# Logs of the gates split into three bfloat16 numbers by GpSimd, their running sums in bfloat16 passes, and the gates' steps moved ahead of the masks

## The chip, the core and the metric

The kernel runs on one core of one Trainium2 chip. The metric is the time of one execution in microseconds on the device, the median of three runs. Everything is computed on one TensorE (matmuls and transposes), one VectorE, one ScalarE and one GpSimd, each with an instruction stream of its own that is worked off in order; the SP queue issues most of the transfers.

## The reference

The first half is a gated linear recurrence with 4 batches, 8 heads, 768 steps and heads of 48:

```python
f = 1.0 / (1.0 + np.exp(-f_logit))
for t in range(S):
    state = f[:, :, t, :, None] * state + np.einsum('bhd,bhe->bhde', k[:, :, t], v[:, :, t])
    y[:, :, t] = np.einsum('bhd,bhde->bhe', q[:, :, t], state)
```

The second half takes y as 3072 rows of 384 and routes each row through two levels of gates (4 groups of 4 experts, both by argmax) to one of 16 experts, relu(x @ w1) @ w2 with a hidden width of 1024, scaled by the product of the two softmax weights:

```python
g_idx = np.argmax(x @ w_group, axis=1)
e_idx = np.argmax(xg @ w_expert[g], axis=1)          # rows xg of group g
out[tok_idx] = combined[:, None] * (np.maximum(xg[mask_e] @ w1[g, e], 0.0) @ w2[g, e])
```

## The kernel before

**The scan.** The 768 steps are cut into 6 chunks of 128, and the 4 batches into 2 pairs. A chunk of one pair of batches is a *unit*; there are 12 of them, numbered 0 to 11, `units[i] = (c, s)`. Each unit goes through stages, each a generator whose `yield`s cut it into steps: `bounded` (c) bounds the gate logits on VectorE; `gated` (g) turns them into logs on ScalarE (an exponential and a log of 128x768, in place, tile ld_f) and then, in two batches (b = 0, 1), forms the running sum of the logs within the chunk on TensorE, a matmul of 128x384 with the triangle of ones `tri` as the stationary operand (tile cs, line 600), and from it two exponentials on ScalarE, eq and kh (lines 601 and 602). The last row of eq is sent by GpSimd's queue to the small tile ends (line 607). `multiplied` (m) multiplies q by eq and k by kh on VectorE (lines 620 and 623); `turned` (t) transposes both on TensorE; `scored` (s) makes the scores ap and masks them on VectorE with `tri` (line 663, four instructions of 128x512, "the masks"); `stated` (n) updates the state (ds, sp, st); `weighed` (w) makes the output y from the state and the masked scores; `done` (d) takes the router's logits lT and lg from it; `listed` (x) transposes the output back to rows; `decayed` (b) turns ends into the decays of a chunk (gt). `routed` (r) ranks the rows of a finished chunk: small VectorE instructions, the matmuls rk and tb, and a transfer (meta, line 246) by GpSimd's queue.

**The order.** TensorE, VectorE, ScalarE and SP run in exactly the order in which the program issues their instructions (`manual_schedule`); only GpSimd's instructions are ordered by the framework. The order is written out as words: `c+2` means the next step of stage c of unit i+2. BEGIN is the order up to unit 2 and the first part of unit 4, and then each of i = 3 to 12 runs through EVEN or ODD, or through an order of its own in ORDERS (the last four). In EVEN and ODD the two sums of unit i+1 stand at `g+1 g+1`, the score steps of unit i at `s s s s`, and the bound, exponential and log of unit i+2 at `c+2`, `g+2` and `g+2`. An iteration of the steady part is about 10.5 to 11.3 us long in the profile.

**After the scan.** Two experts are worked on while the scan ends (`early`), and then the experts one after another: gathered rows, transposes, `up` (hp, line 439), `down` (yo, line 475) and scattered rows. The change does not touch this part.

Of the kernel before, what the change touches and what calls it, by code (L numbers as in the profile page):

```python
# [10 lines left out]
FP32 = mybir.dt.float32  # L11
I32 = mybir.dt.int32
U32 = mybir.dt.uint32
BF16 = mybir.dt.bfloat16
AF = mybir.ActivationFunctionType
OP = mybir.AluOpType
AX = mybir.AxisListType.X
ET = mybir.EngineType
P = 128
# [4 lines left out]
def kernel(  # L24
# [12 lines left out]
    nc = tc.nc  # L37
    B, H, S, D = q.shape
# [38 lines left out]
    def const(shape, dtype, name):  # L77
        return cp.tile(shape, dtype, tag=name, name=name)

    def bank(shape, name):  # L80
        return ps.tile(shape, FP32, tag="bank", name=name)
# [8 lines left out]
    tri = const([P, P], FP32, "tri")  # L90
    ident = const([P, P], FP32, "ident")
    strictb = const([P, P], BF16, "strictb")
    onesb = const([P, P], BF16, "onesb")
    halves = const([P, 2], FP32, "halves")
    make_upper_triangular(nc, tri, val=1.0, diag=True)
    make_identity(nc, ident)
    nc.vector.memset(onesb, 1.0)
    nc.vector.tensor_tensor(strictb, tri, ident, OP.subtract)

# [286 lines left out]
    def fetch(pool, rows, n, top=N, late=False):  # L388

        w = {"n": n, "pool": pool, "early": top < N, "late": late, "blocks": [(j, min(P, n - j * P)) for j in range((n + P - 1) // P)]}  # L390
        w["x"] = pool.tile([P, len(w["blocks"]), RW], FP32, tag="xg", bufs=2 if pool is ep else 6, name="xg")
        for j, m in w["blocks"]:
            nc.gpsimd.indirect_dma_start(out=w["x"][:, j, :], out_offset=None, in_=x_dram[0:1 + top, :], in_offset=bass.IndirectOffsetOnAxis(ap=rows[:, j:j + 1], axis=0))  # L393
        return w
# [124 lines left out]
    with ExitStack() as fast:  # L519
        sb = fast.enter_context(tc.tile_pool(name="sb", bufs=2))  # L520
# [26 lines left out]
        NU = len(units)  # L547
# [9 lines left out]
        def side(i):  # L557


            return nc.gpsimd if i < NU - 2 else nc.scalar  # L560
# [3 lines left out]
        def parts(i):  # L564

            return (slice(0, 1), slice(1, 2)) if i == 0 else (slice(0, 2),)
# [10 lines left out]
        def bounded(i):  # L577
# [3 lines left out]
                nc.vector.tensor_scalar(f, f, -44.0, None, OP.max)  # L581
            yield

        def gated(i):

            c, s = units[i]
            w = live[i]

            nl = w["f"].rearrange("p b h d -> p b (h d)")
            for b in parts(i):  # L590
                nc.scalar.activation(nl[:, b], nl[:, b], AF.Exp, bias=0.0, scale=-1.0)
                if i:
                    yield
                nc.scalar.activation(nl[:, b], nl[:, b], AF.Ln, bias=1.0, scale=1.0)  # L594
            eq, qh, kh = pads["eq"][i % 2], w["qh"], pads["kh"][i % 3]
            w.update(eq=eq, kh=kh)
            yield
            for b in range(2):
                cs = bank([P, H, D], "cs")
                nc.tensor.matmul(cs.rearrange("t h d -> t (h d)"), lhsT=tri, rhs=nl[:, b], start=True, stop=True)  # L600
                nc.scalar.activation(eq[:, b, :, 0:D], cs, AF.Exp, bias=0.0, scale=-1.0)  # L601
                nc.scalar.activation(kh[:, b, :, 0:D], cs, AF.Exp, bias=0.0, scale=1.0)
                if b:

                    if s == 0:
                        ends[c] = sb.tile([B, H * DP], FP32, tag="ends", bufs=1, name="ends")
                    side(i).dma_start(out=ends[c][2 * s:2 * s + 2, :], in_=eq[P - 1:P].rearrange("o b h d -> o b (h d)"))  # L607
                yield
# [171 lines left out]
        def advance(gens):  # L780
# [6 lines left out]


        STAGES = {"c": bounded, "g": gated, "m": multiplied, "t": turned, "s": scored, "n": stated, "w": weighed, "d": done, "x": listed, "b": decayed}
        BEGIN = """c0 h g0 p g0 g0 m0 m0 m0 m0 l2 t0 t0 t0 t0 c1 g1 g1 s0 s0 s0 s0 g1 g1 p w0 w0 n0 m1 m1 m1 m1 l3 h x0 x0 x0  # L790
            t1 t1 t1 t1 b1 c2 g2 g2 s1 s1 s1 s1 p d0 g2 g2 n0 n1 w1 w1 m2 m2 l4 n1
            d0 x1 x1 t2 t2 t2 t2 c3 g3 g3 x1 s2 s2 s2 s2 w2 g3 g3 d1 w2 n2 m3 m3 c4 g4 g4""".split()
        BEGUN = 3
        EVEN = "l+2 d-2 n-1 r r r x-1 x-1 t t t t g+1 g+1 x-1 r s s s s c+2 w d-1 g+2 w g+2 n m+1 m+1".split()
        ODD = "l+2 d-2 r r x-1 x-1 t t t t b n-1 g+1 g+1 x-1 r s s s s c+2 w d-1 g+2 w g+2 n m+1 m+1 r n".split()
        ORDERS = {
            NU - 3: "l+2 o d-2 r r x-1 x-1 t t t t b n-1 r g+1 g+1 x-1 r s s s s c+2 w d-1 g+2 w g+2 n m+1 m+1 r n".split(),
            NU - 2: "d-2 r x-1 x-1 r t t t t r g+1 g+1 x-1 s s s s w d-1 w n m+1 m+1".split(),
            NU - 1: "d-2 r r n-1 x-1 x-1 t t t t r x-1 r s s s s w b d-1 w r r".split(),
            NU: "d-2 r e d-1 x-1 x-1 d-1 x-1 r r r e e r e r r e r r e r e r r e e e e e".split(),  # L800
# [3 lines left out]
        def step(nm, i):  # L804
            if nm == "r":
                advance(routes)
            elif nm == "e":
                next(first[0], None)
            elif nm == "p":
                next(pad)  # L810
            elif nm == "o":
                send_kept()
            elif nm == "h":
                next(turning)
            elif 0 <= i < NU:
                if nm == "l":

                    load(i, ("k", "qh"))
                    if i + 1 < NU:
                        load(i + 1, ("f",))  # L820
                    load(i, ("v",))
                    return
                if (nm, i) not in steps_of:
                    steps_of[nm, i] = STAGES[nm](i)
                next(steps_of[nm, i], None)
# [11 lines left out]
        for i in range(BEGUN, NU + 1):  # L837
            if i == BEGUN:
                nc.sync.dma_start(out=x_dram[0:1, 0:DM].rearrange("o (h d) -> o h d", d=D), in_=blank[:, 0:D].unsqueeze(1).broadcast_to((1, H, D)))
                nc.sync.dma_start(out=x_dram[0:1, DM:RW], in_=blank[:, D:D + 2])  # L840
            for tok in ORDERS.get(i, ODD if i % 2 else EVEN):
                step(tok[0], i + int(tok[1:] or 0))
# [62 lines left out]
    for n in range(GE - 1):  # L905
        w = ws[n]
# [105 lines left out]
    with tc.If(more > 0), ExitStack() as late:  # L1012
# [5 lines left out]
        with tc.For_i(0, last, 1) as i:  # L1018
# [14 lines left out]
            w = fetch(ep, row, P, late=True)  # L1033
# [32 lines left out]
```

## Time and profile before

| | us |
|---|---|
| median of 3 runs | 418.97 (418.01 to 419.13) |
| the profiled execution | 418.8 |
| span of the profile | 416.9 |
| TensorE busy | 404.8 (97%) |
| VectorE busy | 266.9 (64%) |
| ScalarE busy | 157.0 (38%) |
| GpSimd busy | 83.3 (20%) |
| matmuls of the running sums (line 600) | 48 passes, 19.7 |

How to read it: PE is TensorE's matmuls, PEld its loads of the stationary operand, DVE VectorE, ACT ScalarE, POOL GpSimd. A float32 matmul shows as two passes, so the 24 sums are 48 rows. The busy slices cut the span into 40 equal parts of 10.4 us; a digit is the busy share in tenths. In the timeline a row is a start in us, a length in us, the engine, the line, the operation, the output and inputs by their names, and in brackets how long the engine had been idle and on whom it waited. The chain of waits follows the end of the program back from what released it to what released that.

### The profile page before, as it was taken

Reading aid. Unit: us, or ns where it says so; the run is one execution under the profiler, and the core shown is the slowest. Engines: PE = TensorE matmul, PEld = TensorE weight load, DVE = VectorE, ACT = ScalarE, POOL = GpSimd, SP = SyncE. Lnnn points to the kernel's source line nnn. Section 1 sums busy time; section 2 is a strip of 40 time slices with the busy share of each in tenths; the row PEclk is TensorE's granted clock in tenths of the full one; section 3 lists DMA queues with packets and bytes.
Section 4 is the critical chain, followed back from the end, with each engine's and each line's share of the span. In section 5 each row is a group of like instructions: output and inputs, shape, how many; then the busy total and the mean of one; then the engine's idle time right before and its main releaser. Section 6 shows DMA issues by size and latency. Waiting matters only on the chain.

```text
span 416.9 us, 10083 instructions
## 1 busy us (share of the span) xinstructions
PE 404.8 (97%) x4055; PEld 376.0 (90%) x4055; DVE 266.9 (64%) x778; ACT 157.0 (38%) x353; POOL 83.3 (20%) x127
## 2 busy tenths in 40 slices
PE   5999999999999999999999999999999999999995
PEld 3888888888878878989999999999999999999992
DVE  5666787878898641550699777495595595594240
ACT  5777766666565412211122131231231231231220
POOL 4000010101012047101041321311322221120230
PEclk9999999999999999999999999999999999999998
DMA  9999997877999739976639476586595696585010
GB/s 166 203 204 203 184 175 140 154 148 156 257 321 382 260 112 360 381 276 232 227 119 326 118 277 232 178 326 181 199 340 138 261 316 194 210 321 161 28 47 25
DMA packets 132121, 88.98 MB, mean 213 GB/s; under 512 B 102630, under 2 KB 122700, under 8 KB 132066
## 3 DMA queue, kind: packets, MB, share of 16 engines
q1 hardware_dynamic: 125666, 75.50, 61.8%
q0 software_dynamic: 5792, 11.92, 9.7%
q10 hardware_dynamic: 608, 0.83, 0.6%
q8 instruction: 34, 0.56, 0.5%
q14 instruction: 21, 0.17, 0.1%
HBM read 78.71 MB, written 9.83 MB: 212 GB/s over the span
## 4 chain that ended last, share of the span: by engine, by line
PE 48%; issue 30%; DMA 9%; POOL 6%; DVE 3%; ACT 2%; POOLq 1%
PE hp L439 12%; PE yo L475 6%; DMA out_dram<-yt,xg 6%; PE y L702 5%; PE ap L660 4%; PE cs L600 4%; PE yo L460 4%; POOL out_dram L450 4%; PE x_ps L743 2%; POOL xg L393 2%; PE tr_q L634 2%; PE tr_k L634 2%; PE ds L677 2%; PE y L698 2%; DMA xg<-x_dram,rows_e 2%
## 5 line engine op out<-in xcount | busy, mean ns | idle before, releaser
L439 PE MATMUL hp<-xe,w 128*128 128x128 f32 (+14 forms) x864 | 138.6, 320 | 0.0
L439 PEld LDWEIGHTS hp<-xe,w 128*128 128x128 f32 x864 | 135.8, 190 | 0.8
L475 PE MATMUL yo<-h,w 128*128 128x230 f32 (+13 forms) x672 | 115.8, 333 | 0.0
L422 DVE STREAM_TRANSPOSE yr<-yT 32x192 f32<-32x192 f32 (+1 forms) x208 | 70.5, 339 | 70.4 <-ACT yT L476 67.8
L475 PEld LDWEIGHTS yo<-h,w 128*128 128x128 f32 x672 | 113.7, 190 | 0.2
L415 DVE STREAM_TRANSPOSE xe<-xg 32x192 f32<-32x192 f32 (+1 forms) x208 | 69.7, 335 | 8.6 <-PE hp L439 5.6
L440 ACT ACTIVATE h<-hp 128x256 f32<-128x256 f32 (+14 forms) x72 | 34.4, 478 | 103.6 <-PE hp L439 103.6
L450 POOL DMA_INDIRECT out_dram<-yt,xg x32 | 34.4, 1075 | 151.3 <-ACT yt L447 145.7
L476 ACT COPY yT<-yo 128x230 f32<-128x230 f32 (+13 forms) x42 | 13.4, 325 | 80.5 <-PE yo L475 80.5
L393 POOL DMA_INDIRECT xg<-x_dram,rows_p x30 | 29.7, 988 | 50.6 <-DMA out_dram<-yt,xg 27.6
L663 DVE TENSOR_TENSOR am<-ap,tri 128x512 f32<-128x512 f32 x48 | 29.8, 681 | 13.3 <-PE ap L660 13.3
L702 PE MATMUL y<-am,v 128*64 128x128 f32 x384 | 24.7, 277 | 0.7 <-issue 0.6
L702 PEld LDWEIGHTS y<-am,v 128*64 128x64 f32 x384 | 20.9, 137 | 4.1 <-issue 2.9
L660 PE MATMUL ap<-Tq,Tk 48*64 48x128 f32 x768 | 23.8, 272 | 0.2 <-ACT Tk L635 0.2
L660 PEld LDWEIGHTS ap<-Tq,Tk 48*64 48x64 f32 x768 | 20.8, 133 | 2.0 <-issue 1.1
L460 PE MATMUL yo<-w,h 128*128 128x384 f32 x64 | 21.3, 486 | 0.0
L600 PE MATMUL cs<-ld_f,tri 128*128 128x384 f32 x48 | 19.7, 536 | 0.4 <-ACT ld_f L594 0.2
L460 PEld LDWEIGHTS yo<-w,h 128*128 128x128 f32 x64 | 11.9, 190 | 7.4
L607 POOL DMA_DIRECT2D ends<-eq x10 | 5.4, 541 | 57.3 <-ACT eq L601 57.3
L447 ACT ACTIVATE yt<-yr,xg 128x384 f32<-128x384 f32 (+13 forms) x26 | 14.4, 604 | 5.4 <-DVE yr L422 5.4
L634 PE MATMUL tr_q<-ident,qh 128*128 128x128 f32 x96 | 15.4, 286 | 0.2 <-DVE qh L620 0.2
L705 ACT COPY xT<-y 128x512 f32<-128x512 f32 x24 | 13.5, 581 | 5.5 <-PE y L702 5.4
(171 smaller groups left out, 367.5 us busy)
## 6 DMA issues: line engine op xcount, KB each, us to landing
w<-in_moe_w_dram SPq DMA_DIRECT2D x34, 1536.0 KB, 10.6
qh<-in_q_dram SPq DMA_DIRECT2D x12, 384.0 KB, 5.0
ld_k<-in_k_dram SPq DMA_DIRECT2D x12, 384.0 KB, 5.9
v<-in_v_dram SPq DMA_DIRECT2D x12, 384.0 KB, 5.9
ld_f<-in_f_logit_dram SPq DMA_DIRECT2D x11, 384.0 KB, 5.7
x_dram<-x_kept SPq DMA_DIRECT2D x2, 1536.0 KB, 11.7
x_dram<-x POOLq DMA_DIRECT2D x2, 384.0 KB, 8.0
x_dram<-x ACTq DMA_DIRECT2D x2, 384.0 KB, 8.6
```

The costliest lines, as they stand in the source:

```text
L393: nc.gpsimd.indirect_dma_start(out=w["x"][:, j, :], out_offset=None, in_=x_dram[0:1 + top, :], in_offset=bass.IndirectOffsetOnAxis(ap=rows ...
L415: squares(w, lambda n, k_, rk, g, rg: nc.vector.transpose(out=xT[rg, 0:n, k_], in_=x[rk, 0:n, g]))
L422: squares(w, lambda n, k_, rk, g, rg: nc.vector.transpose(out=y[rk, 0:n, g], in_=yT[rg, 0:n, k_]))
L439: nc.tensor.matmul(hp[:, o, :], lhsT=w1[:, ko, (f + o) * P:(f + o + 1) * P], rhs=w["xT"][:, ko, :], start=(ko == 0), stop=(ko == KO - 1))
L440: nc.scalar.activation(h[:, f:f + 2, :], hp, AF.Relu)
L450: sent = nc.gpsimd.indirect_dma_start(out=out, out_offset=bass.IndirectOffsetOnAxis(ap=w["x"][0:m, j, DM + 1:RW].bitcast(U32), axis=0), in ...
L460: nc.tensor.matmul(yp, lhsT=w["h"][:, fo, :], rhs=w2[:, fo, :], start=(fo == 0), stop=(fo == FO - 1))
L475: nc.tensor.matmul(yp, lhsT=w2[:, fo, m * P:(m + 1) * P], rhs=w["h"][:, fo, :], start=(fo == 0), stop=(fo == FO - 1))
L600: nc.tensor.matmul(cs.rearrange("t h d -> t (h d)"), lhsT=tri, rhs=nl[:, b], start=True, stop=True)
L634: nc.tensor.transpose(out=pt[:, a, :], in_=w[nm + "h"][:, b, 2 * a:2 * a + 2, :].rearrange("t r d -> t (r d)"), identity=ident)
L660: nc.tensor.matmul(ap[r][half, a, :], lhsT=w["Tk"][rows, b, a, half], rhs=w["Tq"][rows, b, a, :], start=True, stop=True)
L702: nc.tensor.matmul(ys[b][DP * h:DP * h + DP, a, :], lhsT=w["v"][:, b, 2 * a + (b ^ h), :], rhs=w["am"][b][:, b ^ h, a, :], start=(c == 0 a ...
```

## The change

The constant `trib` is the triangle of ones in bfloat16. For the units from 2 on (`i > 1`), GpSimd splits the logs after ScalarE has made them. The upper half of a float32 word, read as bfloat16, is the number cut off after eight bits; `upper` is a view of these halves, every second bfloat16 of the tile. GpSimd subtracts it from the log (`less`, float32), and then the upper half of `less` from `less` (`least`, bfloat16), which leaves no rest. The sum of a batch is then three bfloat16 matmuls into the same bank, with `upper(nl)`, `upper(less)` and `least`, in place of one float32 matmul. Units 0 and 1 keep the float32 sum.

In EVEN, ODD and the order of iteration 9 (NU - 3), `c+2` moves from behind the masks to the place before `g+1 g+1`, and the two steps `g+2 g+2` from the places around `w` to the place after the first step of `s`, which is ahead of the masks. BEGIN and the last three orders stay.

```diff
--- before.py
+++ after.py
@@ -91,11 +91,13 @@
     ident = const([P, P], FP32, "ident")
     strictb = const([P, P], BF16, "strictb")
     onesb = const([P, P], BF16, "onesb")
+    trib = const([P, P], BF16, "trib")
     halves = const([P, 2], FP32, "halves")
     make_upper_triangular(nc, tri, val=1.0, diag=True)
     make_identity(nc, ident)
     nc.vector.memset(onesb, 1.0)
     nc.vector.tensor_tensor(strictb, tri, ident, OP.subtract)
+    nc.vector.tensor_copy(trib, tri)
 
 
 
@@ -581,6 +583,10 @@
                 nc.vector.tensor_scalar(f, f, -44.0, None, OP.max)
             yield
 
+        def upper(t):
+
+            return t.bitcast(BF16).rearrange("p b (x w) -> p b x w", w=2)[:, :, :, 1]
+
         def gated(i):
 
             c, s = units[i]
@@ -592,12 +598,20 @@
                 if i:
                     yield
                 nc.scalar.activation(nl[:, b], nl[:, b], AF.Ln, bias=1.0, scale=1.0)
+            pieces = [nl]
+            if i > 1:
+                less = sb.tile([P, 2, H * D], FP32, tag="less", bufs=1, name="less")
+                least = sb.tile([P, 2, H * D], BF16, tag="least", bufs=2, name="least")
+                nc.gpsimd.tensor_tensor(less, nl, upper(nl), OP.subtract)
+                nc.gpsimd.tensor_tensor(least, less, upper(less), OP.subtract)
+                pieces = [upper(nl), upper(less), least]
             eq, qh, kh = pads["eq"][i % 2], w["qh"], pads["kh"][i % 3]
             w.update(eq=eq, kh=kh)
             yield
             for b in range(2):
                 cs = bank([P, H, D], "cs")
-                nc.tensor.matmul(cs.rearrange("t h d -> t (h d)"), lhsT=tri, rhs=nl[:, b], start=True, stop=True)
+                for n, piece in enumerate(pieces):
+                    nc.tensor.matmul(cs.rearrange("t h d -> t (h d)"), lhsT=trib if i > 1 else tri, rhs=piece[:, b], start=(n == 0), stop=(n == len(pieces) - 1))
                 nc.scalar.activation(eq[:, b, :, 0:D], cs, AF.Exp, bias=0.0, scale=-1.0)
                 nc.scalar.activation(kh[:, b, :, 0:D], cs, AF.Exp, bias=0.0, scale=1.0)
                 if b:
@@ -791,10 +805,10 @@
             t1 t1 t1 t1 b1 c2 g2 g2 s1 s1 s1 s1 p d0 g2 g2 n0 n1 w1 w1 m2 m2 l4 n1
             d0 x1 x1 t2 t2 t2 t2 c3 g3 g3 x1 s2 s2 s2 s2 w2 g3 g3 d1 w2 n2 m3 m3 c4 g4 g4""".split()
         BEGUN = 3
-        EVEN = "l+2 d-2 n-1 r r r x-1 x-1 t t t t g+1 g+1 x-1 r s s s s c+2 w d-1 g+2 w g+2 n m+1 m+1".split()
-        ODD = "l+2 d-2 r r x-1 x-1 t t t t b n-1 g+1 g+1 x-1 r s s s s c+2 w d-1 g+2 w g+2 n m+1 m+1 r n".split()
+        EVEN = "l+2 d-2 n-1 r r r x-1 x-1 t t t t c+2 g+1 g+1 x-1 r s g+2 g+2 s s s w d-1 w n m+1 m+1".split()
+        ODD = "l+2 d-2 r r x-1 x-1 t t t t b n-1 c+2 g+1 g+1 x-1 r s g+2 g+2 s s s w d-1 w n m+1 m+1 r n".split()
         ORDERS = {
-            NU - 3: "l+2 o d-2 r r x-1 x-1 t t t t b n-1 r g+1 g+1 x-1 r s s s s c+2 w d-1 g+2 w g+2 n m+1 m+1 r n".split(),
+            NU - 3: "l+2 o d-2 r r x-1 x-1 t t t t b n-1 r c+2 g+1 g+1 x-1 r s g+2 g+2 s s s w d-1 w n m+1 m+1 r n".split(),
             NU - 2: "d-2 r x-1 x-1 r t t t t r g+1 g+1 x-1 s s s s w d-1 w n m+1 m+1".split(),
             NU - 1: "d-2 r r n-1 x-1 x-1 t t t t r x-1 r s s s s w b d-1 w r r".split(),
             NU: "d-2 r e d-1 x-1 x-1 d-1 x-1 r r r e e r e r r e r r e r e r r e e e e e".split(),
```

## The prediction

> **What bounds the kernel now.** I read the busy slices first, then the chain of waits through the scan, then the timeline around the log sums, and last the groups by shape for prices.
>
> ```profile
> PE   5999999999999999999999999999999999999995
> DVE  5666787878898641550699777495595595594240
> POOL 4000010101012047101041321311322221120230
> ```
>
> TensorE is busy from the second slice to the last; GpSimd is almost free up to slice 13, that is during the scan. VectorE stands at 0.7 to 0.9 there, so it is near its limit too. In the chain of waits the scan is a row of TensorE pieces that touch one another (start, length, line):
>
> ```profile
> 23.63 0.57 PE lT L718 x16
> 24.20 1.49 PE cs L600 x4
> ...
> 34.43 1.49 PE cs L600 x4
> ...
> 53.19 1.29 PE cs L600 x4
> ```
>
> A unit's sum of logs is two float32 matmuls, which are four passes of 384 columns: 1.29 us back to back, 0.322 a pass. TensorE saved in the scan is time saved, and TensorE made to wait there is time lost: behind the scan, from 165 to 400 us, it is busy in all 235 us, so nothing takes a delay up.
>
> The timeline shows when the logs of units 2, 3 and 4 are ready (start, length):
>
> ```profile
> 23.01 0.84 ACT L594 ACTIVATE ld_f<-ld_f 128x768 f32<-128x768 f32 x1
> ...
> 33.17 0.84 ACT L594 ACTIVATE ld_f<-ld_f 128x768 f32<-128x768 f32 x1
> ...
> 39.81 0.84 ACT L594 ACTIVATE ld_f<-ld_f 128x768 f32<-128x768 f32 x1
> ```
>
> They end at 23.85, 34.01 and 40.65; their sums start at 24.20, 34.43 and 42.53. In the first two units there is 0.35 to 0.42 us between the log and its matmul, and the change puts two GpSimd instructions there.
>
> **The subtractions.** Each of ten units (2 to 11) gets two, 128x768, two inputs and one output, the second needing the first. No such instruction is in the trace. The nearest rows (mean ns is the figure after the busy time):
>
> ```profile
> L888 POOL MEMSET yT<- 128x384 f32 x2 | 0.8, 437 | 0.0
> masks.py:66 POOL TENSOR_SCALAR_AFFINE_SELECT tri<-tri 128x128 f32<-128x128 f32 x1 | 0.3, 282 | 0.0
> masks.py:65 POOL MEMSET tri<- 128x128 f32 x1 | 0.2, 204 | 0.3 <-POOLq L1052 0.3
> ```
>
> Writing costs (437-204)/256 = 0.91 ns an element and 0.09 us fixed. With one input it is (282-90)/128 = 1.5 ns, so an input adds 0.6. Floor: writing alone, 0.09+768x0.91 = 0.79 us. Two inputs: 0.09+768x(1.5+0.6) = 1.7; I take 1.76, a little over because one operand is half-words with a gap. Ceiling: each input as dear as the whole one-input instruction, 0.09+768x3.1 = 2.5. A pair: 1.6, **3.5**, 5.0 us.
>
> **The passes.** Six bfloat16 passes take the place of four float32 ones. Bfloat16 rows exist only up to 64 columns:
>
> ```profile
> L205 PE MATMUL rk<-ohe,onesb 128*128 128x64 bf16 x6 | 1.2, 193 | 0.0
> L205 PE MATMUL rk<-ohe,onesb 128*128 128x16 bf16 x6 | 1.0, 170 | 0.0
> ```
>
> The slope is 23/48 = 0.48 ns a column, 0.184 us for 384. Ends: half a float32 pass, 0.161, if the bytes read set it; a whole one, 0.322, if the gaps between the half-words cost as much as the words. I take 0.184: 1.10 us a unit for 1.29, **0.19 saved**. The weights (98 ns a load) hide behind the passes, as the 190 ns loads do now. The Trainium skill, TensorE: Matmul & The Clock Gate, "Back-to-back issue gap", gives a column a cycle, 162.5 ns for such a pass; by it the saving would be 0.31 a unit and the whole sum 1.1 us lower (7x0.12 and 3x0.09 at the start).
>
> **Start of the scan.** The order is written out there and did not move, so TensorE stands. The first piece of the first batch can run, the third needs the second subtraction; behind that four passes are left, 0.74 us.
> - Unit 2: 23.85+3.52+0.74 = 28.1 in place of 25.69: **+2.4**. Behind it stand ds, y and all of the next unit.
> - Unit 3, on the clock of unit 2: 34.01+3.52+0.74 = 38.3 for 35.92: **+2.35**.
> - Unit 4: the exponentials of unit 3 end 2.2 late (38.8 for 36.57) and VectorE's qh, kh and bound and ScalarE's two passes queue behind them, so its log ends at 42.85; +3.52+0.74 = 47.1 for 44.02+2.35: **+0.75**.
>
> Together +5.5; with pairs of 1.6 us it is 0.48+0.41-0.19 = +0.7, with 5.0 it is +9.9.
>
> **Units 5 to 11.** The saving stands: 7 x 0.19 = **-1.3**. The pieces are early enough: in the iteration of 96 us a log would end at 101 (below), the pair at 104.5, and TensorE wants the next sums at 107. A pair of 5.0 would still fit.
>
> **What moves.** ScalarE's exponential and log (1.7 us) go into its wait for lT (2.50 us, 98.94 to 101.43); in the even iterations the bound, now behind the meta product, ends at 99.2, so the log ends at 100.95 and lgT is not late. Cost nothing; without that gap it would be 1.7 us on lgT and so on lg. The xT copies no longer stand behind the exponential, but nobody waited for them. The bound (0.47 net) moves ahead of the masks: in odd iterations into 1.56 us in which VectorE waits for ap, in even ones to 98.7, so that the table's sum and the masks behind it end at 101.8; y's last half wants them at 101.9 (102.24 now, less the 0.38 that two sums save). In iteration 9 they are late already (y waited 0.16 and 0.35 for them behind the ranking): **+0.5** there. Loads from SP stay in place. On GpSimd's queue the ends transfer (0.52) and the meta transfer (0.79) come out ahead of the pair; behind it stands only the next unit's. If a pair came out ahead of ends, that would land 3.5 us later than now (100.06 and a median of 3.7), with 3.2 to spare before gt at 106.98. The new tile less shares its buffer with the ranking's tile of that name; the ranking of iteration 9 comes at 109.69, behind the sums that read it: nothing. The copy to trib is one small VectorE instruction before the first load lands: nothing.
>
> **GpSimd beside VectorE.** VectorE has no room between the masks of an odd and an even iteration (start, length; the last bracket is its whole idle time from 91.0 on):
>
> ```profile
> 91.02 0.55 DVE L581 TENSOR_SCALAR ld_f<-ld_f 128x768 f32<-128x768 f32 x1
> ...
> 96.88 0.49 DVE L233 TENSOR_TENSOR val<-head,part 128x128 bf16<-128x128 f32 x2
> ...
> 97.73 0.28 PE L251 MATMUL tb<-val,ln 128*128 128x64 bf16 x4
> ...
> 99.08 0.69 DVE L663 TENSOR_TENSOR am<-ap,tri 128x512 f32<-128x512 f32 x1 [0.23 <-PE ap L660]
> ```
>
> The tb matmuls wait for val, with 0.36 us to spare; the bound that leaves this stretch adds 0.47, TensorE's saving takes 0.38: 0.45. Does a subtraction stop VectorE? The only row of both at work (a 128x128 difference of two SBUF tiles at 1.70 us, 0.29 long, beside an iota) shows nothing, but an iota reads nothing. So the delay is 0 at one end; at the other VectorE stands for what is left of the first subtraction after the masks (ready at 90.3, masks done 91.1: 0.95) and all of the second: 2.7. I take 0.95, one running instruction: 0.95-0.45 = 0.5 in each of four pairs of iterations, **+2.0** (0 to 9.0). The Trainium skill speaks against the change here: SBUF — State Buffer, "Who interferes with whom", says that a VectorE instruction with two SBUF inputs and a GpSimd instruction that reads SBUF exclude one another for the whole instruction. By it the q and k products would lie behind the pair and the cost would be at the upper end; no run here shows it.
>
> **Sum.** The profiled execution took 418.8 us (span 416.9 and 1.9 around it; the median of three is 418.97): 418.8+5.5-1.3+0.5+2.0 = **425.5**.
>
> **Rivals.**
> - *Cheap subtractions, faster.* At 0.79 us each and 0.161 a pass, the start costs 0.39+0.32-0.32 and the rest gains 2.2: 418.8-1.8 = 417.0; at 0.184 a pass 418.2. It decides where a pair takes under 1.9 us (2x1.9-2.27 = 1.3+0.19). For it: GpSimd is idle and writes at 0.9 ns. Against: two inputs on an engine where one adds 0.6.
> - *VectorE becomes the bound.* Delay 2.7: 9.0 for 2.0, 432.5. For it: 0.23 us idle in 8. Against: the one row of both.
> - *The passes save nothing.* 0.322 each: 1.93 a unit, +4.5 for -1.3 and 3x0.55 at the start: 433. The change would then not do what it says. For it: no wide bfloat16 row exists.
>
> **Numbers.** Forecast with its own ends (421 to 430) 0.50, cheap subtractions 0.20, VectorE 0.22, passes 0.08. Range 417.0 to 433.0, the ends of the rivals; what is left out is dearer pieces added up. A measurement tells about 0.3% (1.26 us) from no change: faster 0.11 (half of the first rival), same 0.11 (its other half and the forecast's fringe), slower 0.78.
>
> **What would show it.** In the profile after: GpSimd rows of about 1.76 us, twenty; TensorE waiting for GpSimd about 2.4 us before the third piece of units 2 and 3 and not in units 5 to 11; passes 162 to 184 ns apart; q and k products longer or later by about 1 us if VectorE is held. I am wrong if a pair takes under 2 us, if TensorE's wait at the start is under 1 us, or if iterations 4 to 10 are shorter by over 0.5 us each.

## The result, and the profile after

The changed kernel takes 431.61 us (median of six runs, 429.33 to 432.44), the kernel before 418.56 us in the six runs beside it: a ratio of 1.032 (95% interval 1.0302 to 1.0339). The profiled execution took 430.9 us with a span of 429.1, 12.2 us more than before. The forecast was 425.5 us with a range of 417.0 to 433.0: the time is slower, as forecast, but the loss is 13 us where 6.7 were forecast (5.5-1.3+0.5+2.0). The time lies outside the forecast's own ends (421 to 430), beside the rival in which VectorE becomes the bound (432.5).

The busy slices of the profile after:

```profile
PE   5977989899998999999999999999999999999994
...
DVE  5673799999999781361199795775875775695240
...
POOL 4033344444521216601112223213213212111230
PEclk9988999999999999999999999999999999999999
```

PE is at 0.7 in slices 3 and 4 and at 0.8 in slices 6, 8 and 13, where it had 0.9 or more. DVE is at 0.9 or more in eight slices running, and POOL works at 0.2 to 0.5 from slice 3 to slice 12. In the last of these rows, the granted clock, slices 3 and 4 stand at 0.8; before, the whole scan had 0.9 or more.

The groups of the page, for what GpSimd got and for VectorE's products of q and k (mean ns follows the busy time):

```profile
L605 POOL TENSOR_TENSOR less<-ld_f 128x768 f32<-128x768 f32 x10 | 14.6, 1464 | 31.2 <-ACT ld_f L600 14.6
...
L634 DVE TENSOR_TENSOR qh<-qh,eq 128x768 f32<-128x768 f32 (+1 forms) x14 | 17.5, 1250 | 6.2 <-ACT eq L615 6.2
...
L637 DVE SCALAR_TENSOR_TENSOR kh<-kh,ld_k 128x768 f32<-128x768 f32 (+1 forms) x14 | 19.2, 1379 | 1.2 <-DMA ld_k<-in_k_dram 1.2
...
L606 POOL TENSOR_TENSOR least<-less 128x768 bf16<-128x768 f32 x10 | 18.2, 1823 | 0.8
```

A subtraction takes 1.47 us, not 1.76: the first has a mean of 1464 ns; the second has 1823, but it is 1.47 in the rows where VectorE does nothing with two inputs. The two products had a mean of 0.95 us at 128x768 before. The first place to look at is the start of the scan, the timeline around the sums of unit 2:

```profile
22.29 0.84 ACT L600 ACTIVATE ld_f<-ld_f 128x768 f32<-128x768 f32 x1
...
23.21 1.47 POOL L605 TENSOR_TENSOR less<-ld_f 128x768 f32<-128x768 f32 x1 [6.66 <-ACT ld_f L600]
...
23.41 0.34 PE L614 MATMUL cs<-ld_f,trib 128*128 128x384 bf16 x1
...
24.73 0.33 PE L614 MATMUL cs<-less,trib 128*128 128x384 bf16 x1 [0.98 <-POOL less L605]
...
24.76 1.48 POOL L606 TENSOR_TENSOR least<-less 128x768 bf16<-128x768 f32 x1
...
26.30 0.48 PE L614 MATMUL cs<-least,trib 128*128 128x384 bf16 x1 [1.24 <-POOL least L606]
```

and the same timeline from there on:

```profile
26.57 0.53 PE L614 MATMUL cs<-ld_f,trib 128*128 128x384 bf16 x1
...
26.90 0.52 PE L614 MATMUL cs<-less,trib 128*128 128x384 bf16 x1
...
27.22 0.52 PE L614 MATMUL cs<-least,trib 128*128 128x384 bf16 x1
...
27.67 1.95 PE L691 MATMUL ds<-v,kh 128*64 128x48 f32 x32
```

The log ends at 23.13, the first piece runs at 23.41, the second waits 0.98 us for GpSimd and the third 1.24 us. Unit 3 shows 0.95 and 1.21 us, unit 4 0.88 us. There is a second thing in these rows: from the third piece on the passes stand 0.32 us apart (26.57, 26.90, 27.22), not 0.165 as in unit 4 (50.37, 50.54, 50.71), and ds takes 1.95 us where it took 1.14. The granted clock from 25 to 32 us was 0.76, and 0.81 from 36 to 42.

The second place is a steady iteration, here the one of unit 7:

```profile
77.19 1.47 POOL L605 TENSOR_TENSOR less<-ld_f 128x768 f32<-128x768 f32 x1 [1.44 <-DVE am L677]
...
77.72 1.76 DVE L634 TENSOR_TENSOR qh<-qh,eq 128x768 f32<-128x768 f32 x1
...
78.74 2.06 POOL L606 TENSOR_TENSOR least<-less 128x768 bf16<-128x768 f32 x1
...
79.40 2.22 DVE L637 SCALAR_TENSOR_TENSOR kh<-kh,ld_k 128x768 f32<-128x768 f32 x1
```

less starts at 77.19 and ends at 78.66; the q product starts at 77.72 but takes 1.76 us in place of 0.95, so that it ends 0.82 us after less; least was let go when less was done and takes 2.06 in place of 1.47; the k product takes 2.22 and ends 0.82 us after least. They go by turns: each of the four ends about as long after the one before as it would take alone. The chain of waits in the same stretch says who pays:

```profile
75.32 0.97 DVE am L677 x2
...
76.52 1.28 DVE am L677 x2
77.80 1.67 DVE qh L634
79.48 2.14 DVE kh L637
...
82.34 0.48 DVE sp L697
...
85.20 0.49 DVE val L235 x2
```

Before, the scan's chain was a row of TensorE pieces that touched one another. Now it runs through VectorE: the masks, the two long products, then the sums of state and the ranking. Over the whole span VectorE's share of the chain went from 3% to 15%. TensorE waits for no piece here: its only waits for GpSimd's pieces are the five in units 2, 3 and 4.

**Where the 12.2 us came from.** The sums of unit 4 ended at 44.02 us before and end at 51.03 now: +7.0 by the end of the written-out start. The sums of unit 11 started 11.84 us later (119.53 and 131.37): +4.8 in the steady iterations. The first product of the early experts starts 11.8 us later (139.4 and 151.2), the end 12.2.

### The profile page after: what moved, and what is told of

It reads as the page before. It is cut to its first block, busy times and chain, and to the rows that moved or that the text cites. A ratio compares the mean times of both kernels' runs of the same rounds, so it can differ in the third digit from the quotient of the medians.

```text
span 429.1 us, 10158 instructions
## 1 busy us (share of the span) xinstructions
PE 405.9 (95%) x4075; PEld 375.1 (87%) x4075; DVE 283.6 (66%) x779; ACT 159.8 (37%) x353; POOL 118.8 (28%) x147
## 4 chain that ended last, share of the span: by engine, by line
PE 30%; issue 30%; DVE 15%; DMA 11%; POOL 8%; ACT 3%; POOLq 1%; SPq 0%; DVEq 0%
PE hp L441 12%; PE yo L477 6%; DMA out_dram<-yt,xg 6%; PE yo L462 4%; POOL out_dram L452 3%; DVE am L677 3%; DVE kh L637 3%; DVE qh L634 3%; DMA w<-in_moe_w_dram 3%; PE cs L614 2%; POOL xg L395 2%; DMA xg<-x_dram,rows_e 2%; PE y L716 1%; POOL least L606 1%; POOL less L605 1%
## 5 line engine op out<-in xcount | busy, mean ns | idle before, releaser
L605 POOL TENSOR_TENSOR less<-ld_f 128x768 f32<-128x768 f32 x10 | 14.6, 1464 | 31.2 <-ACT ld_f L600 14.6
L634 DVE TENSOR_TENSOR qh<-qh,eq 128x768 f32<-128x768 f32 (+1 forms) x14 | 17.5, 1250 | 6.2 <-ACT eq L615 6.2
L637 DVE SCALAR_TENSOR_TENSOR kh<-kh,ld_k 128x768 f32<-128x768 f32 (+1 forms) x14 | 19.2, 1379 | 1.2 <-DMA ld_k<-in_k_dram 1.2
L606 POOL TENSOR_TENSOR least<-less 128x768 bf16<-128x768 f32 x10 | 18.2, 1823 | 0.8
```

The source lines that it names most:

```text
L637: nc.vector.scalar_tensor_tensor(out=t, in0=t, scalar=math.exp(SAFE), in1=heads(w["k"][:, b]), op0=OP.min, op1=OP.mult)
```

## The experiments

My theory was that the loss has two separate parts, TensorE's wait for the pair at the start (forecast +5.5, with the passes already in it) and the hold of VectorE by GpSimd in the steady part (forecast +2.0), and that the steps' moves cost next to nothing and the bfloat16 passes save 0.19 us a unit. The rivals: the order itself costs; GpSimd's work loads the memory in general, whatever it does; the loss in the steady part is the wait for pieces (the profile after shows no such wait in units 5 to 11).

Each ratio below is to the kernel before in runs beside the run in question; by the group of runs that kernel took 418.0 to 422.9 us (medians), so that only ratios can be compared. The expectations in us are for 418.6, and where a ratio is given in us below, it is of 418.6.

**The two parts by themselves.** Three runs take the change apart by the units that are split.

```diff
@@ split from unit 5, both places @@
-            if i > 1:
+            if i > 4:
@@ the start alone, both places @@
+            if 1 < i < 5:
@@ the order alone: no unit is split @@
+            if i > 99:
```

*From unit 5 on.* 

> Units 2, 3 and 4 keep the float32 sum; units 5 to 11 are split as in the change, in the changed order. The theory (the start of the scan costs 7.0 of the 12.2 us of the two profiles, by the wait for GpSimd and by TensorE's clock after it; VectorE held by GpSimd's reads costs the other 5) expects the start as before and the rest as after: 418.6 + 5 = 423 to 424.5, q and k products still 1.7 and 2.1 us long in the iterations from 3 on. The rival (one cause in the steady part, the start only shifts what would be lost anyway) expects 429 to 431.

Measured: 1.0136 (1.0097 to 1.0176), that is 424.3 us; the q and k products of units 4 to 9 take 1.6 to 1.8 and 2.22 us.

*The start alone.* 

> Only units 2, 3 and 4 are split, 5 to 11 keep the float32 sum, in the changed order. The theory (the start costs 7 of the 12 us) expects a ratio of 1.014 to 1.018 to before (6 to 7.5 us), TensorE waiting 2.2 us in units 2 and 3 and half its clock behind that. The rival (what the start loses would have been lost to VectorE later anyway) expects 1.005 or less.

Measured: 1.0182 (1.0151 to 1.0213).

*The order alone.* 

> No unit is split; only the order of bound, exponential and log is that of the change. The theory (GpSimd's reads hold VectorE, the order alone costs next to nothing) expects 418 to 419.5 and q and k products of 0.95 us. The rival (the bound in front of the masks and the logs in front of lT make VectorE and ScalarE late) expects 422 to 424.

Measured: 0.9997 (0.9974 to 1.0019); its products of q and k are back at 0.95 us:

```profile
L637 DVE SCALAR_TENSOR_TENSOR kh<-kh,ld_k 128x768 f32<-128x768 f32 x8 | 7.6, 950 | 0.0
L634 DVE TENSOR_TENSOR qh<-qh,eq 128x768 f32<-128x768 f32 x8 | 7.6, 947 | 0.0
```

So the order is free, and the two parts add up: 0.0182 and 0.0136 make 0.0318, the change 0.032. In microseconds of 418.6 the start costs 7.6 and the rest 5.7.

**What the rest is made of.** In the run split from unit 5 the starts of successive q products stand 11.99, 10.55, 12.19, 10.54 and 12.19 us apart (from 47.13 us on); with the order alone 10.45, 10.99, 10.46, 10.99 and 10.45. An iteration whose VectorE is full of ranking (a full one) is 1.5 to 1.7 us longer, and the next one, a light one, wins back 0.45. Three runs ask which property of the pair does this.

*Only writes.* Each subtraction is replaced by two memsets of the same output:

```diff
-                nc.gpsimd.tensor_tensor(less, nl, upper(nl), OP.subtract)
-                nc.gpsimd.tensor_tensor(least, less, upper(less), OP.subtract)
+                for _ in range(2):
+                    nc.gpsimd.memset(less, 0.0)
+                for _ in range(2):
+                    nc.gpsimd.memset(least, 0.0)
```

> As the change, but each of the two subtractions is replaced by two writes of zeros over its output, so that GpSimd is busy for about as long, without reading, and only the upper half of each log is summed. The writes wait for no log, so the start should not wait either. The theory (it is GpSimd's reads that hold VectorE) expects q and k products of 0.95 us and 415 to 418. The rival (any work of GpSimd on SBUF holds VectorE) expects products of 1.5 us and more and 422 to 425.

Measured: 1.0039 (1.0014 to 1.0065). The first half of the expectation holds, the time does not. The groups of the stretch from 40 to 130 us:

```profile
L639 DVE SCALAR_TENSOR_TENSOR kh<-kh,ld_k 128x768 f32<-128x768 f32 x8 | 7.6, 950 | 0.0
L636 DVE TENSOR_TENSOR qh<-qh,eq 128x768 f32<-128x768 f32 x8 | 7.6, 946 | 0.0
L583 DVE TENSOR_SCALAR ld_f<-ld_f 128x768 f32<-128x768 f32 x8 | 6.3, 785 | 0.0
```

Thirty-four memsets lie between 27 and 112 us, all but two of them of 0.73 to 0.79 us, and the products stay at 0.95 us, one too that has a memset wholly inside it (80.73 and 80.80 us): writing does not hold an instruction with two inputs. But the bound (one input, float32, in and out in SBUF) has a mean of 785 ns in place of 554, and at the start of the program, where nothing makes the memsets wait, it is far worse. The timeline there:

```profile
3.88 0.73 POOL L606 MEMSET less<- 128x768 f32 x1
3.98 3.77 DVE L583 TENSOR_SCALAR ld_f<-ld_f 128x384 f32<-128x384 f32 x2 [0.77 <-DMA ld_f<-in_f_logit_dram]
...
4.64 0.86 POOL L608 MEMSET least<- 128x768 bf16 x1
...
5.46 0.73 POOL L606 MEMSET less<- 128x768 f32 x1
```

The first two bounds, 0.36 us each before, take 3.77 us together. So this run lost 2.4 us at its start (the first scores began at 13.94 us, with the order alone at 11.54), which the passes then won back (the scores of unit 9 at 107.51 and 107.81). The miss is that second hold, which I had not thought of: writes hold the bound, reads hold the products. Without its 2.4 us the run would be at about 417.8 us, inside the expectation (an estimate).

*On VectorE itself.* The split from unit 5, with both subtractions on VectorE as a stage of their own behind the products:

```diff
+        def split(i):
+            if i > 4:
+                nl, less, least = live[i]["split"]
+                nc.vector.tensor_tensor(less, nl, upper(nl), OP.subtract)
+                nc.vector.tensor_tensor(least, less, upper(less), OP.subtract)
+            yield
...
-... m+1 m+1
+... m+1 m+1 k+2
```

> As e1_from5, but VectorE makes the two subtractions itself, behind the q and k products. That adds 2 x 0.87 us to VectorE in each iteration and takes away the holds of 0.8 and 1.3 us. The theory (the holds are the cost of the steady part) expects products of 0.95 us and a little less than e1_from5: a ratio of 1.008 to 1.013 to before, for 1.0136. The rival (the three passes or the order cost, not the holds) expects 1.018 or more, since VectorE only gets more to do.

Measured: 1.0105 (1.0065 to 1.0145). The subtractions in the stretch from 40 to 130 us:

```profile
L628 DVE TENSOR_TENSOR least<-less 128x768 bf16<-128x768 f32 x7 | 6.7, 958 | 0.2
L627 DVE TENSOR_TENSOR less<-ld_f 128x768 f32<-128x768 f32 x7 | 6.6, 948 | 0.0
```

VectorE needs 0.95 us for each, 1.9 us for the pair, and the products stay at 0.95. GpSimd's pair delays VectorE by 2.1 us an iteration (0.81 in the q product, 1.27 in the k product). So the work that was moved to an idle engine costs VectorE what it would cost there; the ratios are 0.003 apart and their intervals overlap.

*Elsewhere in the iteration.* The split from unit 5 again, with the bound, exponential and log a step earlier, so that the pair lies beside the masks; least is written into the lower halves of the log's tile, and less has two buffers:

```diff
-        EVEN = "l+2 d-2 n-1 r r r x-1 x-1 t t t t c+2 g+1 g+1 x-1 r s g+2 g+2 s s s w d-1 w n m+1 m+1".split()
-        ODD = "l+2 d-2 r r x-1 x-1 t t t t b n-1 c+2 g+1 g+1 x-1 r s g+2 g+2 s s s w d-1 w n m+1 m+1 r n".split()
+        EVEN = "l+2 d-2 n-1 c+2 r r r x-1 x-1 t t t t g+2 g+2 g+1 g+1 x-1 r s s s s w d-1 w n m+1 m+1".split()
+        ODD = "l+2 d-2 r r x-1 x-1 c+2 t t t t b n-1 g+2 g+2 g+1 g+1 x-1 r s s s s w d-1 w n m+1 m+1 r n".split()
```

> Units 5 to 11 split, as in the run that split from unit 5, but with the exponential and log of unit i+2 ahead of the sums of unit i+1, so that GpSimd's pair lies beside the masks (one input in PSUM, one in SBUF) and is over before the q and k products. Theory (only products with two SBUF inputs are held): q and k products back to 0.95 to 1.2 us, masks at 0.69 each, and the time 0.994 to 0.999 of before: the saving of the passes alone (0.996 when tried without any subtraction). Rival (a GpSimd subtraction costs the scan wherever it lies): masks longer than 0.8 us each, 1.008 or more.

Measured: 1.0053 (1.0036 to 1.0069), between the two theories. The order of this run by itself, all sums in float32:

> The order of the run before alone, all sums in float32 and no subtraction: 0.998 to 1.006; it tells what the longer way of eq and kh (two passes of ScalarE ahead of them) costs by itself.

Measured: 0.9981 (0.9955 to 1.0008). The timeline of the masks run, first a light iteration:

```profile
87.42 1.47 POOL L605 TENSOR_TENSOR less<-ld_f 128x768 f32<-128x768 f32 x1 [5.40 <-ACT ld_f L600]
87.51 2.49 DVE L677 TENSOR_TENSOR am<-ap,tri 128x512 f32<-128x512 f32 x4 [1.19 <-PE ap L674]
...
89.91 1.33 DVE L634 TENSOR_TENSOR qh<-qh,eq 128x768 f32<-128x768 f32 x1
...
91.17 0.94 DVE L637 SCALAR_TENSOR_TENSOR kh<-kh,ld_k 128x768 f32<-128x768 f32 x1
```

and the full iteration:

```profile
100.63 2.11 POOL L606 TENSOR_TENSOR ld_f<-less 128x768 bf16<-128x768 f32 x1
101.33 2.22 DVE L637 SCALAR_TENSOR_TENSOR kh<-kh,ld_k 128x768 f32<-128x768 f32 x1
```

The masks beside less take 0.69 us each, as always: one input comes from PSUM, and GpSimd's reads don't hold them. In the light iteration the pair touches only the first 0.5 us of the q product (1.33). In the full one the meta transfer stands ahead of the pair on GpSimd's queue (98.24 to 99.04), least starts a little before the k product, and that stands until it is done: 2.22. Up to unit 9 the q products of this run keep pace with those of its order alone (100.46 and 100.47 there, 26.63 and 26.15 at unit 2), so the split had won 0.5 us by then. It lost most in one place, iteration 9, where GpSimd's pair now lies beside the ranking of the early experts:

```profile
109.59 0.88 DVE L282 TENSOR_TENSOR order<-rank,experts 128x32 f32<-128x32 f32 x1
...
110.93 1.11 DVE L291 CAST who<-names 1x2 int32<-1x2 f32 x1
...
111.96 2.47 DVE L677 TENSOR_TENSOR am<-ap,tri 128x512 f32<-128x512 f32 x4
...
112.69 0.43 PE L716 MATMUL y<-am,v 128*64 128x128 f32 x2 [1.70 <-DVE am L677]
```

The order, a comparison of 128x32 with two inputs, takes 0.88 us beside less, the cast of two numbers 1.11 us beside least. With the order alone they take 0.19 and 0.16. The masks start at 111.96 in place of 110.31, and TensorE waits 1.70 us for them. The last run takes this pair away:

```diff
-            if i > 4:
+            if 4 < i < 11:
```

> The order of the masks run with units 5 to 10 split and unit 11 summed in float32, so that GpSimd does nothing beside the ranking of iteration 9, where the masks run lost: there the order and the cast of the list took 0.88 and 1.11 us beside the pair, 0.19 and 0.16 without it, the masks started 1.65 us later and TensorE waited 1.70 us for them. Theory (that one place gave back more than the whole split had gained): q product of unit 10 about 112.3 (114.36 in the masks run, 112.71 with the order alone), 0.995 to 0.999 of before, so below the masks run's 1.0053 by 2 to 4 us. Rival (the loss came from the pairs of the other iterations): 1.002 or more.

Measured: 1.0004 (0.9992 to 1.0015), 0.0049 below the masks run, that is 2.1 us, and the ranking is undisturbed:

```profile
109.67 0.19 DVE L282 TENSOR_TENSOR order<-rank,experts 128x32 f32<-128x32 f32 x1
...
110.31 0.16 DVE L291 CAST who<-names 1x2 int32<-1x2 f32 x1
110.39 2.46 DVE L677 TENSOR_TENSOR am<-ap,tri 128x512 f32<-128x512 f32 x4
```

The q product of unit 10 starts at 112.78 (expected 112.3). One pair in iteration 9 was most of what the masks run lost. Six split units now cost nothing that can be measured, and they gain nothing either: the interval leaves out the 0.995 to 0.999 that I had expected. Against their own order, 0.9981 (0.9955 to 1.0008), they may still cost about 1 us; the two intervals do not settle it.

**The order of before.** The split with the steps where they stood:

```diff
-        EVEN = "... t t t t c+2 g+1 g+1 x-1 r s g+2 g+2 s s s w d-1 w n m+1 m+1".split()
+        EVEN = "... t t t t g+1 g+1 x-1 r s s s s c+2 w d-1 g+2 w g+2 n m+1 m+1".split()
```

> The split of the change in the order of before. The log of a unit then ends only in the last part of an iteration, about 3 us before its sum. The theory (GpSimd's two subtractions take 3 to 3.5 us behind the log and hold VectorE) expects TensorE to wait 1 to 2 us for them in every iteration on top of the holds: a ratio to before of 1.035 to 1.05, more than the change itself (1.032). The rival (the moved order is what costs) expects less than 1.025.

Measured: 1.0474 (1.045 to 1.0499). The ratio is the expected one, but only in part for the expected reason, so it is partly luck. From unit 4 on TensorE waits for a piece only in units 4, 5, 7 and 9, 0.6 to 1.1 us each, and the q and k products take 0.95 us. The pair lies elsewhere here and holds other instructions on the chain of waits: the state's sum st takes 1.67 us (at 82.58 us) where it takes 0.56 undisturbed, and two small steps of the router, dl and oh, 1.32 and 1.51 us (from 95.02 us) for 0.24. The moves don't speed up the kernel of before, but a split without them would have cost 0.015 more.

**The passes alone.** The order of before, and in place of the second and third piece a constant of zeros:

```diff
-                nc.gpsimd.tensor_tensor(less, nl, upper(nl), OP.subtract)
-                nc.gpsimd.tensor_tensor(least, less, upper(less), OP.subtract)
-                pieces = [upper(nl), upper(less), least]
+                pieces = [upper(nl), none, none]
```

> The order of before; the sums of units 2 to 11 are three bfloat16 passes a batch, but the second and third take a constant tile of zeros, so that only the upper half of each log is summed and GpSimd and VectorE have no part in it. The theory (a pass is 0.165 us in the profile after, so a unit saves 0.3 us of TensorE, and TensorE is what ends the scan) expects 3 us less: 415 to 416. The rival (something else ends the scan as soon as TensorE is faster) expects 418 to 419.

Measured: 0.9962 (0.9939 to 0.9985), 1.6 us where 3 were expected. In the scan the saving is there. Against the profile before, which has the same order, the q product of unit 11 starts 4.57 us earlier (119.96 and 124.53); 0.85 of that stands at the scores of unit 1 already (20.81 and 21.65), ahead of the first split sum. That leaves 3.7 us, 0.37 for each of ten units; the passes' own rows give 0.30 (six at 0.165 in place of four at 0.322). The first product of the early experts is 3.9 us ahead (135.5 and 139.4), or 3.0 without the 0.85. So the 3 us reach the end of the scan in this trace, and the time shows 1.6 (0.6 to 2.6). The two profiles come from different groups of runs, in which the kernel before took 422.3 and 418.97 us, so they can't be compared behind the scan, and where the rest goes stays open.

**The clock at the start.** Two runs fill TensorE's wait with matmuls of zeros into the same bank, ahead of the first piece, which then overwrites them:

```diff
+                for _ in range({2: 18, 3: 18, 4: 8}.get(i, 0) if b == 0 else 0):
+                    nc.tensor.matmul(cs.rearrange("t h d -> t (h d)"), lhsT=trib, rhs=none, start=True, stop=True)
```

The kernel of the first run splits only units 2 to 4, so its partner is the run of the start alone, and not the change that its expectation names.

> The change as it is, and in units 2, 3 and 4 TensorE works on matmuls of zeros (18, 18 and 8 of 384 columns, 0.16 us each) ahead of the first sum, while it would wait for GpSimd; they go into the same bank, which the first piece then overwrites. They take about the time of the wait. The theory (after a wait of 1 us and another of 1.2 TensorE runs at half its clock for about 3 us, twice) expects the clock to stay at 1.0 and the ratio to before to fall from 1.032 to 1.023 to 1.027. The rival (the clock has another cause, or only the waits cost) expects 1.032 or more.

Measured: 1.0169 (1.0131 to 1.0207); its partner has 1.0182, so the times don't tell them apart. The second is the change with the fillers:

> The change as it is, with 18, 18 and 8 matmuls of zeros ahead of the first piece of units 2, 3 and 4, in the place where TensorE waits for GpSimd. Theory (part of the loss at the start is the halved clock behind the waits): granted clock 0.97 or more from 25 to 50 us, scan 1.0 to 1.7 us ahead of the change's, 1.028 to 1.030 of before. Rival (the wait alone counts): the change's 1.032 or more.

Measured: 1.0296 (1.0248 to 1.0345), and the change 1.032 (1.0302 to 1.0339): not apart either. The traces are. The window from 25 to 32 us (busy time of each engine, then the granted clock, which is the number behind the brackets), of the change:

```profile
25.00:32.00 7.00, 5.76 (x74) 4.41 (x72) 4.75 (x12) 2.89 (x6) 1.79 (x2) 0.76 1.10 214
```

and of the change with fillers:

```profile
25.00:32.00 7.00, 7.00 (x93) 5.29 (x91) 5.44 (x15) 3.29 (x7) 2.04 (x3) 1.00 1.15 224
```

With TensorE kept at work the clock is 1.00, the passes of unit 2 stand 0.165 us apart and ds takes 1.14.

But such a pair of waits doesn't always bring the slow clock. In the run in the order of before, TensorE waits 0.99 and 1.24 us in unit 2 as well, yet the passes behind stand 0.165 us apart (27.18, 27.35 and 27.52), ds takes 1.14, and the same window has

```profile
25.00:32.00 7.00, 5.31 (x80) 4.21 (x80) 5.82 (x16) 3.29 (x7) 2.43 (x3) 1.00 1.10 218
```

In its unit 3, behind 0.95 and 1.22 us, the passes are 0.32 us apart again. So the clock fell behind five of the six such pairs in the three traces that have them (the change, the start alone and this one). What decides it, no run shows.

With the fillers, the q products from unit 4 to unit 11 start 1.4 us earlier than in the change (53.21 and 54.62; 134.63 and 136.01), although the fillers hold the third piece of unit 2 up until 27.01, 0.43 us behind the end of least at 26.58 (0.06 in the change). In the change's trace the wait at the start costs more than its own length.

## Why the prediction was right, and where its terms were off

- **Sign and mechanism.** GpSimd's pair on TensorE's way in units 2, 3 and 4, and VectorE held by it later, are the two causes of the loss; taken one at a time they cost 1.0182 and 1.0136. The moves of the steps, forecast at +0.5, cost nothing that can be measured. The time lies in the range because the range went as far as the rivals.
- **The subtraction**: forecast 1.76 us, measured 1.47. The rule for the second input (0.6 ns an element on top of 1.5) was too high: 1.47 us is 1.9 ns an element.
- **The passes**: 0.184 us forecast, 0.165 measured, near the lower end (0.161). A unit saves 0.30 us and not 0.19.
- **The start**: forecast +5.5, measured +7.6 (the run of the start alone) or +7.0 in the traces, where unit 1 was already 0.7 ahead (0.6 at the q product of unit 2 with the order alone). With the true pair (2.94 us) and passes my own formula gives only about 3.5. In the trace, 2.89, 2.84 and 1.39 us go by from the first piece to the third in units 2, 3 and 4, where two passes need 0.33: 6.1 us in all, and three cheaper sums take off 0.9. So the waits alone are 1.7 us dearer than the formula gives them. The rest is the clock, which the prediction left out. In this trace the four passes behind a wait and ds or lT ran at half speed; against the fillers run, from the third piece to the start of what follows was 1.37 us in place of 0.76, and ds 1.95 in place of 1.14, 1.4 us at unit 2, and about 1 us at unit 3. 6.1-0.9+2.4 = 7.6, an estimate. The forecast was not further off because the missing terms stood against a pair that was too dear: that is luck.
- **GpSimd beside VectorE** is the step that failed in size. I took "0.95, one running instruction" against an upper end of 2.7. Measured, the hold is 2.1 us an iteration, because q and k products lie behind both subtractions in turn. The rest of the scan was to cost -1.3+0.5+2.0 = +1.2; it costs 5.7, although the passes save 0.8 more than forecast. That the full iterations pay and the light ones have room was right: 1.5 to 1.7 us in one, 0.45 back in the next. Two pairs of a full and a light iteration lost 1.1 and 1.3 us net of the 0.6 that their passes saved, which makes 1.7 and 1.9 for the hold (an estimate): near the rival's 2.7-0.45 = 2.25, far from my 0.5. The third full iteration lost 1.7, iteration 9 behind it won nothing back, and iteration 10 lost 0.4. That makes 4.4 us by the q product of unit 11. Another 1.1 came between there and the first product of the experts (143.02 us, and 137.32 with the order alone), and 1.0 of it lies in one row: the scores of unit 11 took 3.56 us in place of 2.53, with TensorE stopping among them for nothing that the profile shows. They took 1.98 in the change, so it is open whether the split has to do with that. My reading that VectorE had 0.23 us idle in that stretch was wrong too: the bracket is the last gap alone, and the gaps add up to 0.7.
- **The evidence that I weighed wrongly.** I read one row (a difference beside an iota, no longer than elsewhere) as a sign against the hold, though an iota reads nothing, as the text itself said. The writes run shows how little that row could say: an instruction that only writes leaves the products alone even for 0.7 us at a time. The rule that I cited, SBUF — State Buffer, "Who interferes with whom" of the Trainium skill, is confirmed in both halves here: reads hold two-input products (2.22 us for 0.95), writes do not (0.95), and the bound, of a kind that the section names as able to take both port pairs, is held by writes (3.77 us for 0.72). Had I priced the step by the rule and not by that row, the sum would have been 432.5. That this is so near 431.6 is partly luck: its start is 2.1 us too small, and its rest of 8.2 us was measured at 5.7.
- **Iteration 9**: the forecast had +0.5 for the bound ahead of the masks. From the q product of unit 9 to that of unit 10 it is 12.24 us before and 12.72 with the order alone: right. That the order costs nothing as a whole comes from other iterations, 0.47 and 0.51 shorter in two of them (11.00 and 10.99 for 11.47 and 11.50), which I had not counted.

## What to carry to other kernels

Before work is given to an idle GpSimd, list what VectorE does in the same microseconds: what reads two operands from SBUF stood, in these runs, until GpSimd's subtraction beside it was done, so the work costs VectorE about what it would cost there, unless it lies beside instructions that take one operand from PSUM. Where a chain of two instructions is put ahead of a matmul on a full TensorE, count the wait and the slow clock that can follow it (here some 1.4 us behind two waits of 1.0 and 1.2; the clock fell in five cases of six). And a saving of 0.3 us a unit on the bound engine is worth having only where its preparation is covered; ask first in which of the hand-ordered places, the start and the one with the ranking, it is not.

## What the runs showed of the hardware that I had not expected

- The granted clock fell after waits of 0.98 and 1.24 us with one pass of 0.33 us between them: 0.76 in the window from 25 to 32 us, passes 0.32 us apart in place of 0.165. After the single wait of 0.88 us in unit 4 the passes stayed at 0.165. A like pair of waits (0.99 and 1.24 us) in the run in the order of before left the clock at 1.00, so the lengths of the waits alone don't decide it. The Trainium skill, TensorE: Matmul & The Clock Gate, "HAM oscillation — how this bites in real kernels", warns of idle gaps over 3.4 us; here much shorter ones, close together, were enough in five cases of six.
- GpSimd's memsets hold VectorE's bound of float32 in SBUF: two of 128x384, 0.36 us each before, took 3.77 us in all.
- The hold reaches the smallest instructions: a cast of two numbers took 1.11 us in place of 0.16 beside GpSimd's subtraction. Not every small one is held: the sum over 32 numbers just ahead of it took 0.17 us beside the same subtraction, as without it.
- The pieces that are every second bfloat16 of a tile and the piece that has no gaps take the same time as moving operands: they start at 50.21 (no gaps), 50.37, 50.54 and 50.71 us in unit 4, 0.165 for 384 columns, half of a float32 pass.
